# Attention, two feed-forward layers on one core: reciprocals and normalising passes moved behind two maxima, ten idle products taken out

## The chip, the cores and the metric

The kernel runs on one core of a Trainium2 chip, in one launch. The metric is the time on the device in microseconds (us); the time of the kernel before is the median of three runs.

## The reference

Three steps follow one another. First attention over 2 batches of 8 heads, 768 positions and a head size of 64: scores are scaled by 1/8, a bias that falls linearly with the distance is added, keys outside the last 96 positions and the first 8 are masked, and a softmax follows.

```python
scores = scale * np.matmul(q, k.transpose(0, 1, 3, 2))
scores = np.where(keep, scores + bias[None], -1000000000.0)
a = np.exp(scores - np.max(scores, axis=-1, keepdims=True))
a = a / (np.sum(a, axis=-1, keepdims=True) + 1e-09)
x = np.matmul(a, v)
```

Then, on the 1536 tokens of 512 values, `h = max(x @ w1, x @ w2, x @ w3)` of 768 columns and `h @ w_out`. Last a gated layer: the rows divided by their root mean square and scaled, `silu(g) * val` with two products of 1536 columns each, and a product back to 512 columns. The queries, keys and values are float32, the weights 64-bit floats.

## The kernel before, in words

**Rounds.** Attention is cut into 24 units: six chunks of 256 queries (two blocks of 128) times four pairs of heads. `steps` (L850) runs 28 rounds, `j` from -3 to 24; the text counts them from 0 as `r = j + 3`, as line 1041 does. A round works on several units at once, as a pipeline: it writes the scores of unit r (L771), the maxima and exponentials of unit r (`exponents`, L784 and L788), the transposes of unit r-2 (L812) and their copies to SBUF (`turned`, block 0 on ScalarE at L819, block 1 on VectorE at L821), the products with the values of unit r-3 (L835) and, on ScalarE, the rounded copy `xt` of their result (`out` at L848). The rest of that result is taken by VectorE at the head of the next round (`out(.., True)`, L846), which reads `xt`.

**Softmax.** For each block and head VectorE adds the bias to the scores, writes them to SBUF and takes the extreme value `nmx` in one operation (L784; four in a round, two for each block). ScalarE takes the exponential and its sum `sm` (L788). `normalise` (L792) then adds 1e-9 to the unit's sums (L796), takes the reciprocal `rs` (L797), both on VectorE, and has GpSimd multiply the four pieces by it (L802), in place. The transposes of the unit, in the round behind, read these pieces. Scores have one buffer per head of the pair, so the scores of a round wait for the maxima of the round before.

**Order.** Inside the loop the queues of TensorE, VectorE, ScalarE and GpSimd carry these operations in the order in which the code issues them. What is written behind the loop may be put among them by the framework's planner on all of these but TensorE.

**Beside attention.** At two points of a round (`yield 0` and `yield 1`, `fast` at L1038 to L1050) a product of zeros with 256 columns is issued on TensorE (`keep_warm`, L369) while `r < WARMR`; it feeds nothing. From round 12 on a half of a product of the first layer (L379) is issued there instead. At the round's end `pace` lets one conversion step run, from round 8 two, from round 12 three. A weight unit is converted from raw 64-bit values in such steps: `scaled` (ScalarE, L137), three bit operations on VectorE (L143, L145, L151), a rounding on ScalarE (L165) and a subtraction on GpSimd (L168).

Of the kernel before, what the change touches and what calls it, by code (L numbers as in the profile page):

```python
# [50 lines left out]
LEAD = 3  # L51


WARMR = 9
WROUND = 1
WMORE = 8
WMOST = 12
# [10 lines left out]
class Later:  # L68
# [6 lines left out]
    def __call__(self, steps, fn, *args):  # L75
        self.queue.setdefault(self.now + steps, []).append((fn, args))
# [648 lines left out]
class FastAttention:  # L725
# [124 lines left out]
    def steps(self):  # L850

        def do(fn, d, *args):
            if 0 <= d < self.n:
                fn(d, *args)

        for d in range(2):  # L860
            self.qk_fetch(d)
        for j in range(-LEAD, self.n + 1):
            do(self.qk_fetch, j + LEAD + 2)

            x, pr = divmod(j + 2, NPAIR)
            if pr < CB and 0 <= x < len(self.chunks):
                self.v_fetch(x, pr)
            do(self.normalise, j + LEAD - 1)
            do(self.out, j - 1, True)
            do(self.scores, j + LEAD)  # L870
            do(self.transposes, j + 1)
            do(self.turned, j + 1, 0)
            do(self.exponents, j + LEAD, 0)
            yield 0
            do(self.exponents, j + LEAD, 1)
            do(self.turned, j + 1, 1)
            for i in range(CB):
                do(self.values, j, i)
            yield 1
            do(self.out, j, False)  # L880
            yield 2
# [134 lines left out]
def fast(tc, io, consts, nlf, ngf):  # L1016
# [5 lines left out]
    with ExitStack() as ctx:  # L1022
# [9 lines left out]
        with ExitStack() as c2:  # L1032
            body.warm_up(c2)
            with manual(FRONT):
                att = FastAttention(body, c2, Masks(tc, c2, nlf, ngf), chunks)
                side, n_side, r = early(), 0, 0
                for part in att.steps():
                    if part < 2:  # L1038

                        c = n_side // 12  # L1040
                        if r < WARMR:
                            body.keep_warm(r)
# [93 lines left out]
```

## Time and profile before

| What | Value |
|---|---|
| Median of 3 runs | 576.55 us (576.35 to 578.2) |
| Profiled execution | 575.32 us, span 573.5 us |
| TensorE busy, matmuls | 561.3 us (98%) |
| VectorE, ScalarE, GpSimd busy | 379.5, 250.4, 241.2 us |
| Products of zeros, L369 | 18, two in each of rounds 0 to 8 |

PE is TensorE, PEld its weight loads, DVE is VectorE, ACT is ScalarE, POOL is GpSimd. The span runs from the first to the last instruction of the profiled execution. A row names the line of the kernel and the tile that is written and those that are read (`out<-in`). In a row of a timeline the figure in brackets is the idle time of the engine before it, with what ended it; an instruction's length includes what it waits for inside the engine. Rows of the timeline merge like instructions that follow one another, and the ends of matmuls are modelled.

### The profile page before, as it was taken

Reading aid. Unit: us, or ns where it says so; the run is one execution under the profiler, and the core shown is the slowest. Engines: PE = TensorE matmul, PEld = TensorE weight load, DVE = VectorE, ACT = ScalarE, POOL = GpSimd, SP = SyncE. Lnnn points to the kernel's source line nnn. Section 1 sums busy time; section 2 is a strip of 40 time slices with the busy share of each in tenths; the row PEclk is TensorE's granted clock in tenths of the full one; section 3 lists DMA queues with packets and bytes.
Section 4 is the critical chain, followed back from the end, with each engine's and each line's share of the span. In section 5 each row is a group of like instructions: output and inputs, shape, how many; then the busy total and the mean of one; then the engine's idle time right before and its main releaser. Section 6 shows DMA issues by size and latency. Waiting matters only on the chain.

```text
span 573.5 us, 9229 instructions
## 1 busy us (share of the span) xinstructions
PE 561.3 (98%) x3316; PEld 508.2 (89%) x3316; DVE 379.5 (66%) x801; ACT 250.4 (44%) x605; POOL 241.2 (42%) x301
## 2 busy tenths in 40 slices
PE   7999999999999999999999999999999999999995
PEld 3778788899999999988899999999999988888884
DVE  5899879519679412267588778888887778752220
ACT  4888676414345011165655444443443335442210
POOL 4556554205155001156737555556666544420000
PEclk9999999999999999999999999999999999999999
DMA  8665663103425200000000222222222205203001
GB/s 299 195 223 205 221 218 115 59 1 96 162 80 199 89 1 0 1 2 1 1 0 1 74 74 74 75 73 74 74 74 74 74 0 155 103 3 128 27 29 42
DMA packets 15895, 48.73 MB, mean 85 GB/s; under 512 B 2016, under 2 KB 2016, under 8 KB 15840
## 3 DMA queue, kind: packets, MB, share of 16 engines
q1 hardware_dynamic: 15840, 48.05, 25.5%
q8 instruction: 28, 0.46, 0.3%
q14 instruction: 27, 0.22, 0.1%
HBM read 44.90 MB, written 3.15 MB: 84 GB/s over the span
## 4 chain that ended last, share of the span: by engine, by line
PE 91%; DVE 4%; POOL 2%; ACT 1%; issue 1%; DMA 1%; SPq 0%; DVEq 0%; ACTq 0%
PE q L500 28%; PE mm L379 27%; PE acc L577 16%; PE mo L426 8%; PE tr L812 4%; PE sc L771 4%; PE av L835 4%; PE tr L460 1%; DVE s L784 1%; DMA ni<-nn 1%; ACT s L788 0%; POOL h L550 0%; POOL op L254 0%; PE idle L369 0%; ACT xb L464 0%
## 5 line engine op out<-in xcount | busy, mean ns | idle before, releaser
L500 PE MATMUL q<-xb,op 128*128 128x384 f32 x1008 | 175.5, 334 | 0.5 <-POOL op L254 0.5
L500 PEld LDWEIGHTS q<-xb,op 128*128 128x128 f32 x1008 | 174.6, 188 | 0.8 <-POOL op L254 0.8
L379 PE MATMUL mm<-xt,w 128*128 128x384 f32 x864 | 157.5, 338 | 0.0
L379 PEld LDWEIGHTS mm<-xt,w 128*128 128x128 f32 x864 | 148.5, 188 | 2.6 <-issue 2.6
L168 POOL TENSOR_TENSOR w<-x,w 128x512 fp32r<-128x512 f32 x36 | 51.2, 1427 | 74.7 <-ACT w L165 74.7
L254 POOL TENSOR_TENSOR op<-s,op 128x256 fp32r<-128x256 f32 x48 | 36.0, 763 | 57.7 <-ACT op L253 57.7
L802 POOL TENSOR_SCALAR s<-s,rs 128x232 f32<-128x232 f32 (+1 forms) x96 | 42.4, 461 | 36.6 <-DVE rs L797 28.0
L396 DVE TENSOR_TENSOR h<-mm,h 128x384 f32<-128x384 f32 x48 | 26.4, 553 | 46.0 <-PE mm L379 45.8
L426 PE MATMUL mo<-w,rst 128*128 128x512 f32 x216 | 52.1, 395 | 0.0
L577 PE MATMUL acc<-w,gst 128*128 128x512 f32 x216 | 49.5, 390 | 1.6 <-POOL w L168 0.8
L577 PEld LDWEIGHTS acc<-w,gst 128*128 128x128 f32 x216 | 40.4, 188 | 10.6 <-POOL w L168 1.2
L788 ACT ACTIVATE s<-s,nmx 128x232 f32<-128x232 f32 (+1 forms) x96 | 44.5, 466 | 11.7 <-DVE nmx L784 11.4
L577 PE MATMUL acc<-w,st 128*128 128x512 f32 x216 | 49.1, 389 | 0.0
L577 PEld LDWEIGHTS acc<-w,st 128*128 128x128 f32 x216 | 40.5, 188 | 8.4
L426 PEld LDWEIGHTS mo<-w,rst 128*128 128x128 f32 x216 | 39.8, 188 | 8.0
L517 DVE TENSOR_TENSOR h<-q,h 128x768 f32<-128x768 f32 (+1 forms) x39 | 34.7, 890 | 3.7 <-PE q L500 3.2
L253 ACT CAST op<-s 128x256 fp32r<-128x256 f32 x48 | 18.2, 402 | 42.2 <-DVE s L234 29.5
L520 ACT ACTIVATE g<-g 128x768 f32<-128x768 f32 (+1 forms) x26 | 20.7, 798 | 34.8 <-DVE g L517 34.8
L784 DVE CUSTOM_DVE_ANT_0 s<-sc,bias 128x232 f32<-128x232 f32 (+1 forms) x96 | 31.9, 375 | 6.1 <-PE sc L771 4.6
L165 ACT CAST w<-x 128x512 fp32r<-128x512 f32 x36 | 22.2, 619 | 26.6 <-DVE x L151 18.3
L771 PE MATMUL sc<-qk 64*128 64x232 f32 (+1 forms) x192 | 27.6, 388 | 2.9 <-DVE nmx L784 1.8
L517 DVE TENSOR_TENSOR g<-q,h 128x768 f32<-128x768 f32 (+1 forms) x13 | 11.6, 894 | 26.9 <-PE q L500 26.9
(102 smaller groups left out, 739.8 us busy)
## 6 DMA issues: line engine op xcount, KB each, us to landing
raw<-wgv SPq DMA_DIRECT2D x24, 512.0 KB, 3.6
raw<-w SPq DMA_DIRECT2D x18, 512.0 KB, 3.8
raw<-wo SPq DMA_DIRECT2D x18, 512.0 KB, 3.6
qk<-qk SPq DMA_DIRECT2D x24, 312.0 KB, 4.1
v<-vwin SPq DMA_DIRECT2D x10, 512.0 KB, 5.2
out<-o SPq DMA_DIRECT2D x12, 256.0 KB, 2.1
v<-vwin SPq DMA_DIRECT2D x2, 256.0 KB, 4.8
gcol<-gcol SPq DMA_DIRECT2D x1, 2.0 KB, 1.8
```

The costliest lines, as they stand in the source:

```text
L168: self.nc.gpsimd.tensor_tensor(out=t[:, 1, :], in0=self.x.pop(i), in1=t[:, 0, :], op=ALU.subtract)
L254: nc.gpsimd.tensor_tensor(out=t[:, 1, :], in0=s, in1=t[:, 0, :], op=ALU.subtract)
L379: self.nc.tensor.matmul(ps, w[:, wi, k * P:(k + 1) * P], x[b][:, k, xi, c0:c0 + C2], start=(i == 0), stop=(i == 3 * KT - 1),)
L396: self.nc.vector.tensor_tensor(out=h, in0=ps, in1=h, op=ALU.max)
L426: self.nc.tensor.matmul(ps, h[:, k % 3, hi, :], w[:, wi, :], start=(k + x == 0), stop=(k == NF1 - 1 and x == 2),)
L500: nc.tensor.matmul(ps, a[:, wi, k * P:(k + 1) * P], self.xb[b][:, j, k, xi, :], start=(i == 0), stop=(i == 5))
L517: nc.vector.tensor_tensor(out=o, in0=ps, in1=x, op=ALU.add)
L577: self.nc.tensor.matmul(ps, of(si), w[:, wi, :], start=(f == LAST[0] and si == 1), stop=(f == LAST[-1] and si == 0 and wi == 0),)
L771: nc.tensor.matmul(sc[j][:, i, :n], qk[r, i * P:(i + 1) * P], qk[r, k0:k0 + n], start=True, stop=True)
L784: nc.vector.tensor_tensor_reduce(out=s[:, j, :n], in0=self.sc[d][j][:, i, :n], in1=self.bias(n, 2 * pr + j), scale=-QK, scalar=3.0e38, op0 ...
L788: nc.scalar.activation(s[:, j, :n], s[:, j, :n], AF.Exp, bias=nmx[:, j:j + 1], scale=-1.0, accum_out=sm[:, i, j:j + 1])
L802: nc.gpsimd.tensor_scalar(s[:, j, :n], s[:, j, :n], rs[:, i, j:j + 1], 1.0, op0=ALU.mult, op1=ALU.mult)
```

## The change

`normalise` for unit r-1 is no longer the first step of a round. It is issued behind the scores, the transposes, block 0's copy and block 0's maxima and exponentials. On VectorE the addition and the reciprocal so stand behind L846 and two of the four L784; on GpSimd nothing of the loop stands between, so its four passes keep their place in its queue and wait for a later reciprocal. On TensorE, ScalarE and the DMA queue no instruction is moved. `WARMR` falls from 9 to 4: the products of zeros run in rounds 0 to 3, and the ten of rounds 4 to 8 are left out.

```diff
--- before.py
+++ after.py
@@ -51,7 +51,7 @@
 LEAD = 3
 
 
-WARMR = 9
+WARMR = 4
 WROUND = 1
 WMORE = 8
 WMOST = 12
@@ -865,12 +865,12 @@
             x, pr = divmod(j + 2, NPAIR)
             if pr < CB and 0 <= x < len(self.chunks):
                 self.v_fetch(x, pr)
-            do(self.normalise, j + LEAD - 1)
             do(self.out, j - 1, True)
             do(self.scores, j + LEAD)
             do(self.transposes, j + 1)
             do(self.turned, j + 1, 0)
             do(self.exponents, j + LEAD, 0)
+            do(self.normalise, j + LEAD - 1)
             yield 0
             do(self.exponents, j + LEAD, 1)
             do(self.turned, j + 1, 1)
```

## Rows read from the trace of the kernel before

**Rows 1.** Busy time by stretch: us, busy (instructions) by engine, granted clock, DMA share, GB/s

```profile
...
12.70:16.10 3.40, 3.40 (x19) 2.49 (x16) 3.01 (x15) 2.43 (x10) 1.62 (x4) 0.50 1.03 415
...
34.10:44.60 10.50, 9.77 (x98) 7.70 (x97) 10.33 (x40) 9.61 (x33) 5.91 (x13) 1.00 0.58 184
44.60:110.00 65.40, 65.40 (x535) 53.55 (x536) 56.08 (x190) 45.20 (x150) 34.75 (x62) 1.00 0.51 172
110.00:570.00 460.00, 455.36 (x2458) 426.79 (x2457) 286.91 (x446) 172.33 (x342) 182.76 (x171) 1.00 0.18 58
...
```

**Rows 2.** Timeline of TensorE: start, length, line, operation, idle before, releaser

```profile
...
41.05 1.37 PE L771 MATMUL sc<-qk 64*128 64x232 f32 x8 [0.61 <-DVE nmx L784]
...
44.59 1.20 PE L771 MATMUL sc<-qk 64*128 64x128 f32 x8
45.72 1.09 PE L812 MATMUL tr<-ident,s 128*128 128x128 f32 x8
...
```

**Rows 3.** Timeline of ScalarE, rounds 7 and 8

```profile
...
31.57 0.19 ACT L788 ACTIVATION_READ_ACCUMULATOR s<-s,nmx 128x1 f32 x1
31.66 0.35 ACT L848 CAST xt<-av 128x256 fp32r<-128x256 f32 x1
32.46 0.58 ACT L819 COPY at<-tr 128x512 f32<-128x512 f32 x1 [0.46 <-PE tr L812]
32.95 0.49 ACT L788 ACTIVATE s<-s,nmx 128x232 f32<-128x232 f32 x1
...
```

**Rows 4.** Timeline of VectorE, rounds 8 and 9

```profile
...
31.79 0.17 DVE L796 TENSOR_SCALAR rs<-sm 128x4 f32<-128x4 f32 x1 [0.50 <-ACT s L788]
31.99 0.18 DVE L797 RECIPROCAL rs<-rs 128x4 f32<-128x4 f32 x1
32.09 0.39 DVE L846 TENSOR_TENSOR xt<-av,xt 128x256 fp32r<-128x256 f32 x1
32.40 0.39 DVE L784 CUSTOM_DVE_ANT_0 s<-sc,bias 128x232 f32<-128x232 f32 x1
...
33.67 0.68 DVE L821 COPY at<-tr 128x512 f32<-128x512 f32 x1
...
35.33 0.16 DVE L796 TENSOR_SCALAR rs<-sm 128x4 f32<-128x4 f32 x1
...
37.81 1.64 DVE L151 SCALAR_TENSOR_TENSOR x<-raw,x 128x512 int32<-128x512 int32 x1
...
```

**Rows 5.** Waits before 46 us: who waited for whom: us, times, longest

```profile
...
DVE rs L796 <- ACT s L788: 2.7, 6, 0.6
...
```

**Rows 6.** Timeline of all engines, round 3

```profile
...
15.80 0.17 DVE L796 TENSOR_SCALAR rs<-sm 128x4 f32<-128x4 f32 x1 [0.26 <-ACT s L788]
...
16.48 0.29 DVE L784 CUSTOM_DVE_ANT_0 s<-sc,bias 128x128 f32<-128x128 f32 x1 [0.30 <-PE sc L771]
...
```

**Rows 7.** Timeline of GpSimd, rounds 8, 9 and 11

```profile
...
32.36 1.76 POOL L802 TENSOR_SCALAR s<-s,rs 128x232 f32<-128x232 f32 x4 [1.31 <-DVE rs L797]
...
37.62 1.28 POOL L168 TENSOR_TENSOR w<-x,w 128x512 fp32r<-128x512 f32 x1
...
43.46 1.76 POOL L802 TENSOR_SCALAR s<-s,rs 128x232 f32<-128x232 f32 x4 [1.77 <-PE tr L812]
...
```

**Rows 8.** Timeline of GpSimd, 92 to 102 us

```profile
...
92.16 3.19 POOL L802 TENSOR_SCALAR s<-s,rs 128x232 f32<-128x232 f32 x4 [0.44 <-PE tr L812]
99.24 1.75 POOL L802 TENSOR_SCALAR s<-s,rs 128x232 f32<-128x232 f32 x4 [3.89 <-DVE rs L797]
```

**Rows 9.** Timeline of VectorE, 92 to 102 us

```profile
...
93.06 0.67 DVE L145 SCALAR_TENSOR_TENSOR x<-raw,x 128x512 int32<-128x512 int32 x1
...
100.55 0.99 DVE L151 SCALAR_TENSOR_TENSOR x<-raw,x 128x512 int32<-128x512 int32 x1
...
```

**Rows 10.** Chain of waits, 0 to 60 us: start, length, what, round 8

```profile
...
32.81 0.11 PE idle L369
...
33.95 0.21 PE idle L369
...
```

## The prediction

> **What bounds the kernel now.** I read three views. First the table of stretches [rows 1]: from 44.6 to 110 us TensorE is busy for 65.40 of 65.40 us and then for 455 of 460, so whatever shifts the start of that part shifts the end of the kernel by about as much. The reader is to see that only the 44 us before it can move, and that VectorE is the fullest engine at the end of these: 10.33 of 10.50 us between 34.1 and 44.6, TensorE 9.77. Second the rows of TensorE around the handover [rows 2]: the scores of round 11 at 41.05 us stand idle for 0.61 us and are released by VectorE's `nmx`, and those of round 12 begin at 44.59 us; after that come products of the first layer in every round and TensorE has no gap. So the question is when VectorE ends the maxima of round 11. Third the rows of ScalarE and VectorE in round 8, side by side [rows 3, 4], to see what VectorE waits for.
>
> **Part 1: the move of the reciprocals and passes.** Before, `normalise` opens a round on VectorE. Its first instruction needs the sums of the last round's four exponentials: in round 8 it starts at 31.79 after 0.50 idle, 0.03 after ScalarE's last sum ends (31.57 + 0.19) [rows 3, 4]. All such waits before 46 us are 2.7 us in six [rows 5]. The change takes this instruction from the head of the queue, and one would book the wait as gain. But the next instruction, `out(.., True)` (L846), reads `xt`, which ScalarE writes right behind those same exponentials: 31.66 + 0.35 = 32.01 [rows 3]. With the same 0.03 it can start at 32.04; it started at 32.09 [rows 4]. So the wait moves to the next instruction and 0.05 us is gained.
>
> Against this: the addition and the reciprocal take 0.30 us of VectorE (31.79 to 32.09), and before they lay inside the time in which L846 could not run anyway. Now they stand behind the first two maxima, after the wait, where nothing covers them. Round 8 laid out again: L846 at 32.04, maxima after 0.31 at 32.35, two of four after 0.64 (33.67 - 32.40 = 1.27 for four) at 32.99, then 0.30, then the other two, and the copy at 33.92 instead of 33.67: 0.25 later. ScalarE does not lose by it at once, as its exponentials take 0.47 each and the second pair is wanted later. VectorE does: round 9's first instruction (35.33) has no idle time before it [rows 4], nor has any until round 12, so 0.25 is carried to 44.59.
>
> Rounds 1 to 3 have no L846 yet. There the maxima wait for the scores: in round 3 the addition stands at 15.80 and the maxima only at 16.48, released by TensorE [rows 6]. Here too the 0.30 were covered and are so no longer; three such rounds give 0 to 0.9 us of delay by round 4. Rounds 4 to 8 go round the loop exponentials, `xt`, L846, maxima, exponentials, and win 0.05 each (0.25) and whatever TensorE held up (below). I take 0.1 as what is left in round 8; ends -0.2 and 0.5.
>
> **Part 2: what the passes now lie beside.** The four passes of GpSimd start 0.37 after the reciprocal does (31.99 to 32.36) and take 1.76 us [rows 4, 7]. Before, the time from the reciprocal to the end of the `at` copy was 0.10 + 0.31 + 1.27 + 0.60 = 2.3 us, so the passes, done after 2.13, lay beside operations that read PSUM. Now it is 0.10 + 0.63 + 0.60 = 1.33 us, and 0.8 us of passes hang over into the conversion steps (L143, L145, L151), which read SBUF alone. What such an overlap costs: the last step of a conversion takes 1.64 us instead of some 0.67 when it starts 0.19 after GpSimd's `w` subtraction, whose end at 38.90 it seems to await [rows 4, 7]; beside the passes that began at 99.24 it was 0.99, that is 0.32 more; and the step at 93.06 lost nothing (0.67), while the four passes beside it took 3.19 us instead of 1.76 [rows 8, 9].
>
> The Trainium skill, "SBUF — State Buffer", section "Who interferes with whom", has VectorE and GpSimd share one port pair as an exclusive lock: whoever issues first holds it for the whole instruction and the other fully blocks. The 1.64 us row agrees, the rows at 93.06 agree only with GpSimd as the loser. By the rule alone every overhang would be lost to whoever comes second, which is rival C.
>
> Up to the handover the steps of rounds 8 and 10 count (those of 4 to 6 fall into loops with idle time of VectorE): 0 to 0.8 each, I take 0.15, the mean of 0 and 0.32, so 0.3. In round 9 the subtraction starts later because the passes do (37.62 before), so its clash with the 1.64 us step may go (-0.97), or it hits round 10's small addition instead, which by its whole length is up to +1.28. The subtraction moves, the clash does not vanish: I take 0 and keep both ends.
>
> **Part 3: transposes behind the passes.** Round 12's transposes stood at 45.72, the passes they need ended at 43.46 + 1.76 = 45.22 [rows 2, 7]. The passes come 1.6 us later (L846 and two maxima, 0.95, and the 0.65 so far), to 46.8; the transposes come 0.65 later, their second half at some 46.9 (half of 1.09 on). They meet almost exactly. If a conversion step holds it up, TensorE waits, and here nothing is slack any more: 0 to 0.6, I take 0.1.
>
> **Part 4: ten products fewer.** They cost 0.11 and 0.21 in a round [rows 10], 0.32 in each of rounds 4 to 8, 1.6 us of TensorE. Their cover is VectorE: at 41.05 TensorE waits 0.61 for it, so time saved earlier is only waited there. They do hold up ScalarE's copy of the transposes (0.46 idle in round 8), but the exponentials of 32.95 also need the maxima begun at 32.40, so they could have started some 0.2 earlier at best (32.40 + 0.32 + 0.03) [rows 3, 4]. That is in the 0.1 of part 1. The clock: in rounds 9 to 11 no such product runs, TensorE is 9.77 of 10.50 us busy and the granted clock is 1.00, 2.4 GHz [rows 1]; I take it that rounds 4 to 8 stay there as well.
>
> **Sum.** 0.25 + 0.1 + 0.3 + 0 + 0.1 = 0.75 us later. Instructions that the planner puts between the loop's own on VectorE after 80 us may come in another order; I count 0, ends ±0.3. The profiled execution took 575.32 us (span 573.5), so 576.07; the median of the runs, 576.55, lies 1.23 above it, so the forecast is 577.3.
>
> **Rivals.**
> A, the forecast: the wait moves by one instruction, its cover is lost. Own range -1.0 (0.25 with the 0.97 clash gone and 0.3 from the planner) to +1.7: 575.5 to 578.2. Chance 0.48.
> B, the wait really goes: the reciprocal was what held the maxima, and L846 is early enough. For it: 2.7 us of waits on ScalarE [rows 5]. Against it: the 32.01 of `xt`. Price: the waits of rounds 4 to 8, three with 0.50 the largest, so 1.5 at most, taken as 1.1, and the 0.97 clash: -2.1, 574.4. Chance 0.18.
> C, slower by the passes: steps and passes wait out one another. Place: rounds 8 to 10. Price: 0.25 + 0.1 as in A, the overhang of 0.8 in full in rounds 8 and 10, and half of 1.28 in round 9 or the transposes: +2.6, 579.1. It decides from about 0.5 us lost in a round. For it: 1.64 against 0.67; against it: the row at 93.06. Chance 0.2.
> D, the clock falls once in rounds 4 to 8: between 12.7 and 16.1 us it was 0.50 (1.2 GHz) after stretches of waiting [rows 1]. Such a 3.4 us stretch loses 1.7 us of work, some 0.3 of it into slack: with A +2.1, 578.7. Against it: rounds 9 to 11. Chance 0.07.
> E, nothing moves, as order and products both lie in others' shadow: 576.5. Chance 0.07.
>
> **How the numbers follow.** What can be told from no change here is 0.3%, 1.7 us: 574.8 and 578.3. Faster: B but for 0.02 and a tail of A of 0.01, 0.17. Slower: C but for 0.03, D but for 0.02, a tail of A of 0.03: 0.25. Within: 0.58. The range leaves out the far halves of B, C and D: 574.4 to 579.3; A's own stands above.
>
> **What would show it.** Right: in the changed profile VectorE's L846 has the idle time that L796 had, ended by ScalarE's `xt`; L796 has none in rounds 4 to 8; the copies L821 of rounds 8 to 11 come 0.2 to 1 us later, counted from 5 us; passes L802 above 1.76 us or steps above 0.7 in rounds 4 to 11; round 12's scores at 45.0 to 45.6. Wrong: L846 without idle time and round 12's scores before 44 us (B); steps of 1.2 us and more in rounds 8 and 10 (C); a second stretch at 0.50 (D). If the scores of round 12 and the end of the kernel move by different amounts, my first claim is wrong.

## The result, and the profile after

The changed kernel takes 579.78 us (median of six runs, 579.51 to 579.87), the kernel before 576.32 beside it (six, 575.39 to 578.2). The ratio is 1.0059 [1.0045, 1.0073] (in brackets, here and below, the 95% interval), so it is slower by 3.4 to 3.5 us. The forecast was 577.3, 0.75 us later, with a range to 579.3: the direction was right, the size lies beyond the range, and a slowdown that can be told had been given a chance of 0.25. The profiled execution takes 579.51 us (span 577.7) against 575.32 (573.5).

**The stretches first.** The first fence is the table of stretches after, with the columns of [rows 1].

```profile
13.60:17.00 3.40, 3.40 (x16) 2.41 (x15) 2.40 (x13) 2.64 (x10) 1.68 (x4) 0.50 1.03 409
34.10:44.60 10.50, 9.79 (x96) 7.45 (x95) 10.33 (x40) 9.72 (x34) 7.22 (x13) 1.00 0.55 173
46.81:110.00 63.19, 61.71 (x499) 49.85 (x500) 58.29 (x185) 44.34 (x147) 35.74 (x60) 1.00 0.50 174
```

VectorE is as full ahead of the handover as it was (10.33 of 10.50). Behind the handover (round 12, where the products of the first layer begin) TensorE now has gaps: 61.71 busy of 63.19 us, where [rows 1] had 65.40 of 65.40. The timeline of TensorE shows two of them.

```profile
46.81 1.20 PE L771 MATMUL sc<-qk 64*128 64x128 f32 x8 [0.50 <-DVE nmx L784]
47.94 0.76 PE L812 MATMUL tr<-ident,s 128*128 128x128 f32 x5
48.90 0.55 PE L812 MATMUL tr<-ident,s 128*128 128x128 f32 x3 [0.19 <-POOL s L802]
...
99.99 1.37 PE L771 MATMUL sc<-qk 64*128 64x232 f32 x8 [1.29 <-DVE nmx L784]
```

Round 12's scores begin at 46.81 (44.59 in [rows 2]), its transposes wait for GpSimd's passes, and round 22's scores wait 1.29 us for VectorE's maxima.

**Where the wait went.** VectorE, with the columns of [rows 4], round 3 and rounds 8 to 10:

```profile
17.35 0.29 DVE L784 CUSTOM_DVE_ANT_0 s<-sc,bias 128x128 f32<-128x128 f32 x1 [1.25 <-PE sc L771]
...
33.41 0.42 DVE L846 TENSOR_TENSOR xt<-av,xt 128x256 fp32r<-128x256 f32 x1 [0.49 <-ACT xt L848]
...
34.39 0.16 DVE L796 TENSOR_SCALAR rs<-sm 128x4 f32<-128x4 f32 x1
34.59 0.18 DVE L797 RECIPROCAL rs<-rs 128x4 f32<-128x4 f32 x1
34.68 0.37 DVE L784 CUSTOM_DVE_ANT_0 s<-sc,bias 128x232 f32<-128x232 f32 x1
...
35.90 0.66 DVE L143 TENSOR_SCALAR x<-x 128x512 int32<-128x512 int32 x1
36.59 0.82 DVE L145 SCALAR_TENSOR_TENSOR x<-raw,x 128x512 int32<-128x512 int32 x1
...
39.81 0.92 DVE L151 SCALAR_TENSOR_TENSOR x<-raw,x 128x512 int32<-128x512 int32 x1
...
41.62 0.70 DVE L796 TENSOR_SCALAR rs<-sm 128x4 f32<-128x4 f32 x1
```

And the waits before 46 us:

```profile
DVE xt L846 <- ACT xt L848: 1.1, 3, 0.5
```

The row of [rows 5], 2.7 us in six waits of L796, is gone. L846 now has three waits on `xt`, in rounds 4, 5 and 8; in round 3, as in [rows 6], the maxima wait for the scores. L796 and L797 now stand between two pairs of maxima, and the conversion steps L143, L145 and L151 are longer (0.66, 0.82, 0.92). In the kernel before, with no GpSimd instruction beside them, the same operations read:

```profile
27.70 0.68 DVE L151 SCALAR_TENSOR_TENSOR x<-raw,x 128x512 int32<-128x512 int32 x1
...
34.27 0.41 DVE L143 TENSOR_SCALAR x<-x 128x512 int32<-128x512 int32 x1
34.72 0.69 DVE L145 SCALAR_TENSOR_TENSOR x<-raw,x 128x512 int32<-128x512 int32 x1
```

ScalarE and GpSimd after:

```profile
33.03 0.34 ACT L848 CAST xt<-av 128x256 fp32r<-128x256 f32 x1
34.10 0.58 ACT L819 COPY at<-tr 128x512 f32<-128x512 f32 x1 [0.72 <-PE tr L812]
34.59 0.49 ACT L788 ACTIVATE s<-s,nmx 128x232 f32<-128x232 f32 x1
```

```profile
38.87 2.19 POOL L802 TENSOR_SCALAR s<-s,rs 128x232 f32<-128x232 f32 x4 [1.99 <-DVE rs L797]
41.03 1.27 POOL L168 TENSOR_TENSOR w<-x,w 128x512 fp32r<-128x512 f32 x1
...
46.65 2.19 POOL L802 TENSOR_SCALAR s<-s,rs 128x232 f32<-128x232 f32 x4 [2.00 <-DVE rs L797]
```

In round 8 ScalarE's copy of the transposes, which stands ahead of the exponentials, waits 0.72 us for TensorE (0.46 in [rows 3]). The passes take 2.19 us beside a step (1.76 in [rows 7]). The subtraction, at 37.62 before, now runs from 41.03 to 42.30 and the addition of four elements in each of 128 partitions, which starts at 41.62, takes 0.70 us and ends with it.

**The sum by rounds.** The rows of TensorE give the start of each round's first score product (L771). Differences of these starts leave out the head, where the stretch at half clock lies elsewhere in each execution. They make the table that everything below uses (us).

| | start r4 | r4 to 6 | r6 to 12 | r12 to 13 | r13 to 17 | r17 to 18 | r18 to 21 | r21 to 22 | r22 to end |
|---|---|---|---|---|---|---|---|---|---|
| before | 18.29 | 5.89 | 20.42 | 5.48 | 19.73 | 4.93 | 15.78 | 5.33 | 477.7 |
| after | 19.00 | 6.25 | 21.56 | 5.88 | 19.73 | 5.10 | 15.78 | 6.69 | 477.7 |

The differences are 0.71, 0.36, 1.14, 0.40, 0.17 and 1.36; together 4.1 of the 4.2 us by which the spans differ. The five kernels below and above that have the new order in rounds 6 to 11 and four rounds of products, with nothing else changed there (after, new_from4, new_upto11, new_4to11, old_only21), take 21.56 to 21.59 for r6 to 12, so such an interval can be read from a single execution.

### The profile page after: what moved, and what is told of

It reads as the page before. It is cut to its first block, busy times and chain, and to the rows that moved or that the text cites. A ratio compares the mean times of both kernels' runs of the same rounds, so it can differ in the third digit from the quotient of the medians.

```text
span 577.7 us, 9209 instructions
## 1 busy us (share of the span) xinstructions
PE 563.1 (97%) x3306; PEld 509.1 (88%) x3306; DVE 384.4 (67%) x801; ACT 251.1 (43%) x605; POOL 245.8 (43%) x301
## 4 chain that ended last, share of the span: by engine, by line
PE 87%; DVE 6%; POOL 2%; ACT 2%; issue 1%; DMA 1%; SPq 0%; DVEq 0%; ACTq 0%; POOLq 0%
PE q L500 28%; PE mm L379 26%; PE acc L577 16%; PE mo L426 8%; PE sc L771 3%; PE tr L812 3%; PE av L835 2%; DVE s L784 2%; PE tr L460 1%; ACT s L788 1%; DMA qk<-qk 1%; DVE x L151 1%; POOL h L550 0%; POOL op L254 0%; DVE at L821 0%
## 5 line engine op out<-in xcount | busy, mean ns | idle before, releaser
L379 PE MATMUL mm<-xt,w 128*128 128x384 f32 x864 | 157.8, 338 | 0.0
L379 PEld LDWEIGHTS mm<-xt,w 128*128 128x128 f32 x864 | 148.5, 188 | 2.8 <-issue 2.6
L168 POOL TENSOR_TENSOR w<-x,w 128x512 fp32r<-128x512 f32 x36 | 53.1, 1479 | 66.7 <-ACT w L165 58.2
L802 POOL TENSOR_SCALAR s<-s,rs 128x232 f32<-128x232 f32 (+1 forms) x96 | 44.2, 479 | 43.9 <-DVE rs L797 27.1
L396 DVE TENSOR_TENSOR h<-mm,h 128x384 f32<-128x384 f32 x48 | 26.3, 549 | 46.2 <-PE mm L379 45.9
L788 ACT ACTIVATE s<-s,nmx 128x232 f32<-128x232 f32 (+1 forms) x96 | 44.6, 467 | 10.8 <-DVE nmx L784 10.0
L784 DVE CUSTOM_DVE_ANT_0 s<-sc,bias 128x232 f32<-128x232 f32 (+1 forms) x96 | 32.5, 372 | 6.9 <-PE sc L771 6.6
L771 PE MATMUL sc<-qk 64*128 64x232 f32 (+1 forms) x192 | 30.0, 394 | 5.0 <-DVE nmx L784 4.0
L771 PEld LDWEIGHTS sc<-qk 64*128 64x128 f32 x192 | 20.0, 202 | 12.2 <-DVE nmx L784 7.0
```

What stands on the lines that cost most here:

```text
L168: self.nc.gpsimd.tensor_tensor(out=t[:, 1, :], in0=self.x.pop(i), in1=t[:, 0, :], op=ALU.subtract)
L379: self.nc.tensor.matmul(ps, w[:, wi, k * P:(k + 1) * P], x[b][:, k, xi, c0:c0 + C2], start=(i == 0), stop=(i == 3 * KT - 1),)
L396: self.nc.vector.tensor_tensor(out=h, in0=ps, in1=h, op=ALU.max)
L771: nc.tensor.matmul(sc[j][:, i, :n], qk[r, i * P:(i + 1) * P], qk[r, k0:k0 + n], start=True, stop=True)
L784: nc.vector.tensor_tensor_reduce(out=s[:, j, :n], in0=self.sc[d][j][:, i, :n], in1=self.bias(n, 2 * pr + j), scale=-QK, scalar=3.0e38, op0 ...
L788: nc.scalar.activation(s[:, j, :n], s[:, j, :n], AF.Exp, bias=nmx[:, j:j + 1], scale=-1.0, accum_out=sm[:, i, j:j + 1])
```

## The experiments

All kernels below are the kernel before with the edit shown. "Old" order is `normalise` at the round's head, "new" is where the change puts it.

**The two parts apart.**

```diff
# products of zeros left out, old order
-WARMR = 9
+WARMR = 4
```

> Only the ten products of zeros of rounds 4 to 8 are left out (WARMR 4); normalise stays at the head of each round. Theory T (the moved instructions cost the time, the products none): as the kernel before, 576.0 to 576.8 us, round 12's scores within 0.4 us of 44.6. Rival P (without the products TensorE falls to its lower clock, or something else hangs on them): at least 578 us, and a second stretch at a granted clock of 0.50.

Measured: 576.34 us, ratio 1.0008 [0.9999, 1.0017], the time as expected. From round 12 on every interval is that of before; rounds 6 to 12 take 20.75 and rounds 4 to 6 5.64, together what they take before. Round 12's scores do not stand near 44.6, as was expected, but at 46.91: this execution was at half clock until 20.8 us, while the products still ran, and began round 4 at 20.52. From round 5 to 11 its granted clock is 1.00.

```diff
# new order, products in nine rounds as before (WARMR = 9)
-            do(self.normalise, j + LEAD - 1)
 ...
             do(self.exponents, j + LEAD, 0)
+            do(self.normalise, j + LEAD - 1)
```

> Only the move; all eighteen products of zeros stay (WARMR 9). Theory T: as the changed kernel, 579.3 to 580.6 us, a little more than 579.8 where the products, 0.32 us a round, stand on TensorE's path in rounds 4 to 8. Rival P: 576.3 to 577.5 us.

Measured: 579.4 us, 1.0062 [1.0049, 1.0076], as expected; rounds 6 to 12 21.50, 12 to 13 5.88, 21 to 22 6.69. The move alone is the whole loss; the ten products do nothing that can be measured.

**The move in some rounds only** (WARMR = 4 in these three and in old_only21).

```diff
-            do(self.normalise, j + LEAD - 1)
+            old = j + LEAD < 4                          # new_from4
+            old = j + LEAD > 11                         # new_upto11
+            old = j + LEAD < 4 or j + LEAD > 11         # new_4to11
+            old = j + LEAD in (21, 22)                  # old_only21
+            if old:
+                do(self.normalise, j + LEAD - 1)
 ...
             do(self.exponents, j + LEAD, 0)
+            if not old:
+                do(self.normalise, j + LEAD - 1)
```

> The changed kernel with the old place of normalise in rounds 0 to 3. Theory T: the 1.15 us by which the copy L821 of round 3 comes later in the changed kernel are the lost cover of the first rounds and are carried to the end; without them 578.0 to 579.2 us, and that copy back at 18.2 to 18.5 us. Rival H (the first rounds' delay would be made up by round 8, as the prediction had it, and the loss arises later): 579.5 to 580.0 us.

Measured: 579.35 us, 1.0057 [1.0043, 1.007], between the two expectations; the copy of round 3 is back at 18.23. By the medians leaving the first three rounds alone wins nothing that can be told. Executions with a like mean clock say more: at 0.996 this kernel took 578.31 and after 579.51 and 579.61, at 0.991 579.35 to 579.72 and 579.72 to 579.87. Its profile has the half-clock stretch where before has it (12.7 to 16.1 us) and round 4 starts at 18.27 (18.29), so here the table can be read without the head: rounds 4 to 12 take 27.46 (26.31), 12 to 13 5.89, 17 to 18 5.09, 21 to 22 6.70; span 576.5, which is 3.0 above before.

> The changed kernel with the old place of normalise from round 12 on. Theory T: in round 21 of the changed kernel two conversion steps (L151) stand between the addition and the reciprocal, ahead of the second maxima, and TensorE waits 1.29 us for round 22's scores; with the old place they stand behind the maxima again. 577.9 to 578.7 us, no idle time over 0.4 us before round 22's scores. Rival S (from round 12 on TensorE has slack for all of it, and 1.29 us is a chance of one execution): 579.4 us and more.

Measured: 577.92 us, 1.0033 [1.0021, 1.0046], as expected. Rounds 6 to 12 take 21.57 and 12 to 13 5.89, but 17 to 18 and 21 to 22 are 4.93 and 5.33 again: about 1.5 us of the change's loss comes from rounds 12 and up (1.9 by the medians).

> The new order in rounds 4 to 11 alone, ten products fewer. By the traces so far rounds 6 to 12 take 1.1 us more, rounds 4 and 5 up to 0.4, and round 12's transposes wait 0.4 for the last passes, so against 575.6 us of the kernel before: 577.0 to 577.7 us. Rival: the rest of the loss hangs together with the other rounds and goes with them, under 576.2 us.

Measured: 577.57 us, 1.0027 [1.0015, 1.0038], as expected. Rounds 6 to 12 take 21.58, 12 to 13 5.88.

**Rounds 21 and 22.** In after, VectorE's rows of round 21 read:

```profile
97.42 0.39 DVE L784 CUSTOM_DVE_ANT_0 s<-sc,bias 128x232 f32<-128x232 f32 x1
97.74 0.16 DVE L796 TENSOR_SCALAR rs<-sm 128x4 f32<-128x4 f32 x1
97.81 1.28 DVE L151 SCALAR_TENSOR_TENSOR x<-raw,x 128x512 int32<-128x512 int32 x2
99.02 0.17 DVE L797 RECIPROCAL rs<-rs 128x4 f32<-128x4 f32 x1
99.10 0.52 DVE L396 TENSOR_TENSOR h<-mm,h 128x384 f32<-128x384 f32 x1
99.55 0.38 DVE L784 CUSTOM_DVE_ANT_0 s<-sc,bias 128x232 f32<-128x232 f32 x1
```

Two conversion steps now stand between the addition and its reciprocal. Inside the loop the code issues these two back to back, so the steps come from behind the loop and were put there by the planner, on VectorE's queue. The second pair of maxima (99.55) waits behind them, and so do round 22's scores (99.99). Before, L796 and L797 stood at the round's head and only an L396 (94.91, 0.55 us) lay between the two pairs. So the theory was the place of the pair in these rounds.

> The changed kernel with the old place of normalise in rounds 21 and 22 alone. Theory S1 (the 1.29 us wait before round 22 is the planner's order: two L151 ahead of the second maxima of round 21): 577.9 to 578.6 us, round 21 to round 22 in 5.3 us and not 6.7. Rival: the reciprocals of all late rounds cost, 579.2 us and more.

Measured: 578.68 us, 1.0042 [1.0028, 1.0057]; 21 to 22 takes 5.33, 17 to 18 still 5.10. Its VectorE and TensorE at that place:

```profile
98.06 0.39 DVE L784 CUSTOM_DVE_ANT_0 s<-sc,bias 128x232 f32<-128x232 f32 x1
98.38 0.54 DVE L396 TENSOR_TENSOR h<-mm,h 128x384 f32<-128x384 f32 x1
98.85 0.38 DVE L784 CUSTOM_DVE_ANT_0 s<-sc,bias 128x232 f32<-128x232 f32 x1
...
99.48 0.68 DVE L151 SCALAR_TENSOR_TENSOR x<-raw,x 128x512 int32<-128x512 int32 x1
```

```profile
99.73 1.05 PE L771 MATMUL sc<-qk 64*128 64x232 f32 x8
```

The step is behind the maxima again and the scores wait for nothing: 1.36 us by the trace, 1.1 by the medians (579.78 and 578.68; the kernel came out 0.1 above its range, and the intervals of the two ratios are wide enough for both).

**What rounds 4 to 11 lose: passes, steps, or the place itself.** In the pairs from here on WARMR is 4, and the new order is that of new_4to11. The pairs without passes, without conversions and without additions ran once each, so it is the intervals of their traces that count. The first pair leaves out the passes (L802) of units 3 to 10, in either order.

```diff
             s = self.s[d, i]
+            if 3 <= d <= 10:
+                continue
```

> The old order with ten products fewer; GpSimd's passes (L802) of units 3 to 10 are left out, so their probabilities stay undivided. Read from the trace: the time from the first scores of round 6 to those of round 12, 20.4 us in the kernel before, 20.75 with only the products out, 21.5 to 21.6 in every kernel with the move in rounds 6 to 11. Theory T: 19.4 to 20.6 us (the subtraction L168 no longer waits behind passes and clashes less).

> As nopass_old (passes of units 3 to 10 left out), with the new order in rounds 4 to 11. Theory T (most of the 1 us of rounds 6 to 11 is the passes lying beside the conversion steps, the lost cover some 0.25): the stretch from round 6 to round 12 at most 0.4 us longer than in nopass_old. Rival O (the order of VectorE's own queue costs it, whatever GpSimd does): at least 0.8 us longer.

Measured: 575.97 and 577.13 us; rounds 6 to 12 take 20.10 and 21.30, so without these passes the new order is still 1.20 later. My theory, which put most of the loss on passes beside steps, missed here (it had at most 0.4); the rival has the number (0.8 or more), but not "whatever GpSimd does". The rows of GpSimd and of VectorE in nopass_new show what took the passes' place:

```profile
37.17 1.28 POOL L168 TENSOR_TENSOR w<-x,w 128x512 fp32r<-128x512 f32 x1 [18.50 <-DVE xt L848]
```

```profile
37.66 0.82 DVE L796 TENSOR_SCALAR rs<-sm 128x4 f32<-128x4 f32 x1
38.51 0.18 DVE L797 RECIPROCAL rs<-rs 128x4 f32<-128x4 f32 x1
```

The subtraction, with no passes ahead of it, falls on the addition, which ends with it (37.66 + 0.82 = 38.48; 37.17 + 1.28 = 38.45), and does so again at 44.93 (0.79). In the old order neither stood there: additions at 36.69 and 43.61 of 0.16 and 0.17. The rounds with these two additions, 9 and 11, hold 0.63 and 0.35 of the 1.20. So this pair removes one overlap and makes another, and doesn't tell what the passes cost.

The second pair has no conversion steps before round 12; what it measures ends there, as the weights come late (589.38 and 591.17 us).

```diff
-WROUND = 1
+WROUND = 12
```

> The old order with ten products fewer and no conversion step before round 12 (they come in a heap there, so only rounds 4 to 11 are to be read). Theory T: VectorE has time over in each round, which is then set by the loop exponentials, xt, L846, maxima: rounds 6 to 12 in some 18.0 to 19.0 us.

> As noconv_old, with the new order in rounds 4 to 11. Theory T (without conversion steps nothing lies beside the passes, and the reciprocals have room): rounds 6 to 12 within -0.4 to +0.2 us of noconv_old, the 0.05 us a round of the prediction as a gain. Rival O: at least 0.8 us longer.

Measured from round 6 to 12: 18.93 and 19.53. With no step and no subtraction at all the new order still loses 0.60, between the two expectations (0.2 at most, 0.8 at least): nothing in round 6 and 0.08 to 0.17 in each of rounds 7 to 11. ScalarE of noconv_new shows the place:

```profile
33.62 0.59 ACT L819 COPY at<-tr 128x512 f32<-128x512 f32 x1 [0.72 <-PE tr L812]
...
36.67 0.59 ACT L819 COPY at<-tr 128x512 f32<-128x512 f32 x1 [0.33 <-PE tr L812]
```

The copy waits 0.72 and 0.33 in turn (0.45 and 0.34 in noconv_old). It needs the transposes, which TensorE takes behind the scores, and these need the second maxima of the round before. That is a loop of its own: second maxima, scores, transposes, copy, exponentials, `xt`, L846, maxima. The 0.30 us of L796 and L797 stand inside it once in every round. That the 0.60 is their price is argued from this; nothing in the pair takes them out.

**The place tested by itself.** The addition is left out for units 3 to 10, in either order.

```diff
-        nc.vector.tensor_scalar(rs, sm, 1e-9, None, op0=ALU.add)
-        nc.vector.reciprocal(rs, rs)
+        if not 3 <= d <= 10:
+            nc.vector.tensor_scalar(rs, sm, 1e-9, None, op0=ALU.add)
+            nc.vector.reciprocal(rs, rs)
+        else:
+            nc.vector.reciprocal(rs, sm)
```

> The order of before with four rounds of products; the addition of 1e-9 (L796) is left out for units 3 to 10, so that the reciprocal reads the sums itself. From the scores of round 6 to those of round 12 this order took 20.42 and 20.75 us with the addition. Theory K (a covered position costs nothing): where ScalarE's last sum is awaited the 0.17 to 0.20 of the addition lie in no one's way; three of the six rounds have no such wait and win 0.2 each: 20.1 to 20.6, that is 0.1 to 0.6 less. Rival M (the small operations cost the same wherever they stand): six times 0.2, 19.2 to 19.6, 1.2 less.

> The new order in rounds 4 to 11 alone, the same addition left out. With the addition 21.50 to 21.59 us from the scores of round 6 to those of round 12. Theory K: here the addition stands in the round's own chain (second maxima, scores, transposes, copy, exponentials) in every round, and where GpSimd's subtraction falls on it that stretch goes as well, unless the reciprocal meets it in its place: 0.8 to 1.4 less, 20.1 to 20.8, and the distance to the old order without the addition shrinks from 0.8-1.1 to 0.5 or less. Rival M: as much less as in the old order, the distance stays 0.8 or more. If what the new order loses sits in the conversion steps beside the passes, little is won in either: 0.3 or less here.

Measured: rounds 6 to 12 take 20.10 and 20.60 (574.41 and 576.37 us). Against old_warm4 and new_4to11 that is 0.65 and 0.98 less, and the distance of the two orders falls from 0.83 to 0.50. VectorE in noadd_old, the same round as in [rows 4]:

```profile
31.27 0.18 DVE L800 RECIPROCAL rs<-sm 128x4 f32<-128x4 f32 x1 [0.50 <-ACT s L788]
```

In the old order rounds 6 to 8 win nothing: in rounds 7 and 8 the sums are awaited as before (0.34 and 0.50; 0.32 and 0.51 with the addition), and round 6 wins nothing without such a wait. Rounds 9, 10 and 11, where L796 has no wait, win 0.20, 0.25 and 0.19. In the new order rounds 6 and 8 win nothing either; in round 8 L846's wait for `xt` grows from 0.49 to 0.69 instead. Rounds 7, 9, 10 and 11 win 0.21, 0.21, 0.27 and 0.29. So, round 6 apart, the addition costs its length or more where no wait covers it and nothing where one does, in either order; the new order pays in four of these six rounds, the old one in three. 0.50 us between the orders remains: the reciprocal still stands there and steps still lie beside passes, and these two were not parted further. The old order won 0.05 more than expected, the new one what was expected. (Lines behind the edit are numbered 3 higher.)

**The wait for `xt`.** In rounds 4 to 11 the products with the values and `xt` are issued ahead of block 1's exponentials, so that ScalarE writes `xt` two exponentials earlier.

```diff
+            early = 4 <= j + LEAD <= 11
+            if early:
+                for i in range(CB):
+                    do(self.values, j, i)
+                do(self.out, j, False)
             do(self.exponents, j + LEAD, 1)
             do(self.turned, j + 1, 1)
 ...        # values and out(j, False) here only if not early
```

> As new_4to11, but in these rounds the products with the values and ScalarE's xt are issued ahead of the second maxima and exponentials, so that L846 has xt long before it starts. Theory L (two chains hold a round: L846's wait on xt, and maxima, scores, transposes, ScalarE's copy, exponentials; the 0.3 us of addition and reciprocal now stand in the second): L846 has no idle time, yet rounds 6 to 12 still take 21.0 to 21.6 us, 576.8 to 577.7 us in all. Rival W (the wait on xt, to which the old wait moved, was what ate the gain): 20.4 us or less, 575.0 to 576.0 us.

Measured with the new order of new_4to11: 576.29 us, 1.001 [1.0, 1.002], rounds 6 to 12 21.09: the rounds as the first theory had them, at the low end, the time 0.5 below it and above the rival's. VectorE's rows of round 8 show that the wait of L846 goes and that the next one follows at once:

```profile
31.37 0.42 DVE L846 TENSOR_TENSOR xt<-av,xt 128x256 fp32r<-128x256 f32 x1
32.05 0.40 DVE L784 CUSTOM_DVE_ANT_0 s<-sc,bias 128x232 f32<-128x232 f32 x1 [0.25 <-PE sc L771]
```

So both loops bind there, one behind the other: 0.49 of the 0.83 against old_warm4 goes with the early `xt`, in rounds 8 and 9, and then the maxima wait for the scores.

> The order of before, but in rounds 4 to 11 the products with the values and the rounded copy xt are issued ahead of block 1's exponentials, as in the run with xt early in the new order (21.09 us over rounds 6 to 12, 576.29). In the old order the sums are what VectorE awaits, and with xt ahead of two exponentials these end 0.35 later. Theory K: the addition so starts up to 0.35 later in the rounds that wait for it, and nothing is won where none does: 20.7 to 21.9 over rounds 6 to 12, 576.0 to 577.3. Rival Y (an early xt helps whatever the order, as TensorE and ScalarE have one link less): as much less as in the new order, 0.3 to 0.6: 20.0 to 20.4, 575.2 to 575.8.

Measured with the old order: 576.5 us, 1.001 [0.9999, 1.0022], rounds 6 to 12 21.27, 0.5 more than without the early `xt`, as the first theory had it. The sums end later, and the addition waits for them:

```profile
32.88 0.17 DVE L796 TENSOR_SCALAR rs<-sm 128x4 f32<-128x4 f32 x1 [0.77 <-ACT s L788]
```

With an early `xt` the new order is thus the better one by 0.18 in the trace, which the medians can't tell; with the late `xt` of both kernels it is the worse one by 0.8 to 1.1.

**The clash of subtraction and step.** In the old order GpSimd's second subtraction is issued one step earlier (WARMR = 9 here), first always, then up to round 10, then up to round 9 (the three edits drawn together).

```diff
             if mid:
                 self.bits(i - 1, 1)
             if new:
                 self.scaled(i)
+            early = self.early        # sub_early: True; sub_r10: r < 11; sub_r9: r < 10
+            if old and early:
+                self.split(i - 2, 1)
             yield
 ...
-            if old:
+            if old and not early:
                 self.split(i - 2, 1)
```

> The kernel before, with GpSimd's subtraction (L168) issued one conversion step earlier, so that in rounds 9 and 11 it runs ahead of the passes and not beside the last bit operation. If that clash (1.64 us against 0.68) is on the path: L151 at 0.7 us in both rounds, rounds 6 to 12 in 19.6 to 20.0 us, 574.7 to 575.3 us against 575.6. Rival: the passes now come later and the transposes wait for them, or the clash falls on another operation: within 0.2 us of the kernel before.

Measured: 575.86 us, 0.9993 [0.998, 1.0005]: the rival, no difference. L151 takes 0.68 in both rounds and rounds 6 to 12 take 19.79, as the theory had it, but 12 to 13 takes 6.08. TensorE and GpSimd at round 12:

```profile
47.20 1.70 PE L812 MATMUL tr<-ident,s 128*128 128x128 f32 x8
```

```profile
44.73 1.28 POOL L168 TENSOR_TENSOR w<-x,w 128x512 fp32r<-128x512 f32 x1 [1.57 <-ACT w L165]
45.99 4.06 POOL L802 TENSOR_SCALAR s<-s,rs 128x232 f32<-128x232 f32 x8
```

A subtraction now stands ahead of the passes that round 12's transposes await (1.70 instead of 1.09 us).

> The kernel before, with GpSimd's second subtraction issued one conversion step earlier up to round 10 alone: one in round 9, while that of round 11 stays behind the passes of round 12's transposes. With both early, rounds 6 to 12 took 19.79 us and the step from round 12 to 13 6.08, where it had been 20.42 to 20.75 and 5.48: 0.6 to 0.9 won, 0.6 given back, since round 12's transposes awaited passes that stood behind the subtraction. Theory K: 12 to 13 is 5.47 to 5.50 again, and 0.2 to 0.5 stay of the gain: 575.3 to 575.9, at best just under the kernel before. Rival: the clash of 1.64 us in round 9 comes back elsewhere in the old order, nothing is left: 575.9 to 576.4.

Measured: 576.0 us, 0.9998 [0.9987, 1.001], 12 to 13 6.00: missed. The step at the end of round 10 is the one to leave alone, and the limit was one round too high.

> As the run with the subtraction early up to round 10, the limit one round lower. That run kept the loss at round 12 (6.00 us to round 13), since the step at the end of round 10 still issued a subtraction ahead of the passes which round 12's transposes await (44.00 1.28, then 45.26 2.19). With the limit at 9 only the subtraction of round 9 is early, whose clash with VectorE's last step (1.64 us) cost 0.97. Theory K: rounds 6 to 12 take 19.8 to 20.1, 12 to 13 takes 5.47 to 5.50: 0.4 to 0.7 below the kernel before on the same chip, ratio 0.9988 to 0.9993. Rival: the late subtraction of round 11 falls on round 12's addition and costs there what was won: ratio 0.9995 to 1.0005.

Measured: 575.14 us against 576.64, 0.998 [0.9968, 0.9992], a version that beats both kernels. Rounds 6 to 12 take 19.77, 12 to 13 5.47, all others as before. By the trace the gain is 0.65 us, in rounds 10 and 11; the ratio says somewhat more than that and than was expected, its interval holds both. VectorE's last step of round 9, 1.64 us in [rows 4], and GpSimd beside it (lines numbered 2 to 5 higher):

```profile
38.97 0.68 DVE L153 SCALAR_TENSOR_TENSOR x<-raw,x 128x512 int32<-128x512 int32 x1
```

```profile
36.97 1.28 POOL L170 TENSOR_TENSOR w<-x,w 128x512 fp32r<-128x512 f32 x1 [1.68 <-PE tr L817]
...
43.98 1.75 POOL L807 TENSOR_SCALAR s<-s,rs 128x232 f32<-128x232 f32 x4 [1.78 <-DVE rs L802]
45.70 1.28 POOL L170 TENSOR_TENSOR w<-x,w 128x512 fp32r<-128x512 f32 x1
```

## Why the prediction was wrong, step by step

**The first claim failed, and with it the largest part of the miss.** That "whatever shifts the start of that part shifts the end of the kernel by about as much" held for before, where TensorE had no gap behind the handover. It was taken as a property of the kernel, and it was one of that order. By the prediction's own test (round 12's scores and the end must move alike) it is wrong: 2.22 and 4.2 us. The scores stood at 46.81, where the forecast had 45.0 to 45.6. The term that was mis-sized is the planner's, 0 with ends of ±0.3; it measured 1.36 in round 21. The 1.36 is shown by old_only21, and its place by the rows. The 0.17 of round 17 is of another kind, as GpSimd's rows before and after show:

```profile
69.92 1.27 POOL L168 TENSOR_TENSOR w<-x,w 128x512 fp32r<-128x512 f32 x1 [3.21 <-ACT w L165]
```

```profile
72.54 1.59 POOL L168 TENSOR_TENSOR w<-x,w 128x512 fp32r<-128x512 f32 x1 [0.80 <-ACT w L165]
```

VectorE's L151 before it ran from 72.31 to 73.00; the subtraction takes 0.32 longer, and the first product with that weight (L379) starts at 74.19, 0.06 behind its end and 0.15 later in its round. The four kernels with the new order in round 17 all have 1.59 to 1.62 there, the kernel before and those with the old order there 1.27 to 1.28. It is an overlap of a step and GpSimd, for which the sum had no term behind the handover.

**Part 1, right in what moves, wrong in what it costs.** The wait did move from L796 to L846, ended by `xt`, and L796 has none in rounds 4 to 11. The step that failed is "ScalarE does not lose by it at once", with the cover of 0.30 us booked once, for round 8, and the other rounds as small gains. ScalarE does lose, by way of scores, transposes and the copy that is queued ahead of its exponentials; without steps and subtractions the order costs 0.08 to 0.17 in each of rounds 7 to 11 (noconv pair). The noadd pair shows a covered and an uncovered place directly (round 7: 0.01 in the old order, 0.21 in the new), but also that the old order was covered in half of these rounds only and that the new one is in some. Rounds 4 to 12 cost 1.15 us in new_from4 where the prediction had 0.25 + 0.1 + 0.3 for parts 1 and 2. What the three rounds of the head cost is not settled: 0.71 us in the two profiles, but with the half-clock stretch in another place; by the ratios of new_from4 and after (1.0057 and 1.0059) nothing that can be told; by executions of like clock 1.2 at 0.996 and some 0.4 at 0.991.

**Part 2, right in kind, too small.** A step beside the passes lost 0.13 to 0.25 us (L143 0.66 against 0.41, L145 0.82 against 0.69, L151 0.92 against 0.68). For rounds 8 and 10 0.15 each was taken; their two steps lost 0.38 and 0.40 together, and steps of rounds 5, 6, 9 and 11 were hit too. What of this reached the path was not measured by itself. The clash of 1.64 us was rightly expected to move and not to vanish: L151 fell to 0.92, and the addition rose to 0.70. The rule of the Trainium skill that was weighed there ("SBUF — State Buffer", "Who interferes with whom") agrees with that addition: it ends when the subtraction does (42.32 and 42.30). Beside the passes both sides lost, the step 0.24 and the passes 0.43 us, and this agrees too once the four passes are taken one by one, as a lock for a whole instruction asks. L151 starts at 39.81 inside the third pass (39.73 to 40.19); the fourth starts at 40.17, inside L151 (to 40.73), and ends at 41.06 after 0.89 instead of 0.46. The section says this of VectorE operations with two inputs in SBUF or in a two-port mode, not of all: the maxima of [rows 4], which read PSUM beside the passes of [rows 7], kept their 0.39.

**Part 3** was 0.1 with an end of 0.6 and measured 0.40. The passes were to come 1.6 later and came 3.19 later (46.65 against 43.46), and they took 2.19 instead of 1.76; the transposes came only 2.22 later (47.94 against 45.72), and their last three wait for the passes.

**Part 4 was right.** old_warm4 can't be told from before, new_warm9 not from after, and the granted clock is 1.00 in rounds 5 to 11 of all these kernels, so rival D is out. B and E are out, as the interval of the ratio lies above 1. C was right in direction and nearest in its time (579.1), but this was luck: no step of 1.2 us stands in rounds 8 and 10, and the largest loss of one round, 1.36, lies in round 21.

## What to carry to other kernels

A small operation that stands where a wait covers it costs nothing, and the same operation between two links of a round's chain is paid for wherever no wait covers it; before it is moved, follow each chain that runs through the new place, by way of other engines' queues too. Where a planner fills the queues, a moved pair can be parted by work that was behind it, at places the old trace shows no gap; look there before calling a part of the kernel closed. Compare kernels by the intervals between like points, here each round's first scores, since the head differs from one execution to the next.

## What the runs showed of the hardware

The stretch of granted clock 0.50 (1.2 GHz) in the head is not a fixed cost of a kernel. Table of stretches of old_warm4, and of noadd_old, whose first three rounds hold the same instructions:

```profile
10.60:14.00 3.40, 2.21 (x15) 1.45 (x16) 2.58 (x17) 2.17 (x9) 1.45 (x4) 1.00 1.03 417
14.00:20.80 6.80, 6.80 (x35) 4.53 (x35) 5.43 (x25) 5.08 (x20) 3.34 (x10) 0.50 0.75 271
```

```profile
9.20:12.60 3.40, 2.22 (x18) 1.34 (x16) 2.24 (x13) 2.42 (x10) 1.62 (x4) 1.00 1.02 418
12.60:16.00 3.40, 2.85 (x22) 1.89 (x20) 3.22 (x16) 2.73 (x10) 1.62 (x4) 1.00 1.03 413
```

After stretches alike (TensorE 2.21 and 2.22 of 3.40 us busy) the one fell to 0.50 for 6.8 us and the other stayed at 1.00; round 4 began at 20.52 and 17.66. That is 2.9 us between two single executions, near the whole effect studied here. One kernel shows it too: of the 16 executions of the kernel before beside old_warm4, those with a mean granted clock of 0.995 to 0.997 took 575.09 to 575.73 us, those with 0.991 or 0.992 576.29 to 577.25. Why one falls and the other doesn't, no run here shows.
